# Chunk preparation, weight order and crossbar transposes in an attention and feed-forward kernel

## The chip, the cores and the metric

The kernel runs on 1 core of one Trainium2 chip. The metric is the device time of one execution in microseconds (us). Of each kernel, several executions were timed, one of them with a profile; the kernel before was run on the same chip beside every experiment.

## The reference, cut to what matters

```python
# q, k, v: (4, 8, 768, 64); heads 0, 2, 6 attend to everything before them,
# the five others to the first 4 tokens and a window of 64
scores = scale * np.matmul(q, k.transpose(0, 1, 3, 2))
scores = np.where(mask, scores, -1e9)
a = np.exp(scores - np.max(scores, axis=-1, keepdims=True))
a = a / (np.sum(a, axis=-1, keepdims=True) + 1e-09)
attn = np.matmul(a, v)
x = attn.transpose(0, 2, 1, 3).reshape(3072, 512)
h = x @ w_in                       # 512 x 2048
out = np.maximum(0.01 * h, h) @ w_out   # 2048 x 512
```

## The kernel before

The 3072 tokens are taken in 8 chunks of 384. For each chunk there is a preparation (k and q transposed), an attention that makes x, a first product with w_in ("product n", 16 ticks of four matmuls), and a second with w_out that makes the out tiles. A slot is a short piece of such work, a tick a slot of four matmuls. Slots of neighbouring chunks are merged, so that TensorE always has something to do; an empty slot only lets time pass. Everything is issued in program order; no scheduler moves it.

GpSimd issues nearly all loads from HBM (SyncE those of the first k, ScalarE a few values of v). SyncE issues transposes by the DMA crossbar, shifted copies of v, and the output. Chunks 1 and 2 are prepared by TensorE transposes; from chunk 3 on k and q go by the crossbar, six transposes in a row, followed by two shifts of v:

```python
def prep_dma(n):
    ...
    for g in range(3):
        nc.sync.dma_start_transpose(out=kt[i]...[:, :, tk], in_=kz[n % 2][:, g]...)      # k step
        nc.sync.dma_start_transpose(out=qts[n][:, :, t], in_=cast["q", n][:, g]...)      # q step
```

The buffers tie the two engines: `kz` has two buffers, so GpSimd may load k of chunk n + 2 only when the k steps of chunk n are through; `qb` has two as well. The main loop, and the choice of who transposes x:

```python
for n in range(2, NCH):
    a = []
    if n + 3 < NCH:
        load(n + 3)                       # GpSimd
    if n + 2 < NCH:
        prep_dma(n + 2)                   # SyncE: six transposes
        v_shift(n + 2, nc.sync)           # SyncE: two shifts
    if n + 1 < NCH:
        late = n + 1 > 3                  # x by crossbar from chunk 4 on
        a = Attention(n + 1, x_dma=late).slots()
        if late:
            a += [lambda: None] * (len(a) // 5)    # empty slots: time for the x transposes
    run(merge(merge(in_slots(n), outs) if outs else in_slots(n), a))
    ...
    outs = out_slots(n, ("py", "pt", "py") if n > 2 else ("py", "py", "py")) ...   # banks: buffers that TensorE writes
```

and the beginning:

```python
load(0, "v")
load_vb0()
masks()                      # GpSimd: eight small operations
for i in range(3):
    load_w("in", i)          # first weights
load(1)                      # k, q, v of chunk 1
load_w("in", 3)
...
in0 = in_slots(0, ("ph", "psS"))
run(in0[0:12])               # 12 ticks of the first product of chunk 0
for j, p in enumerate((0, 1, 3, 2)):
    prep_pair(1, p, ("py", "pt")[j % 2], "vva")    # TensorE transposes k and q of chunk 1
    ...
run(merge(out0[0:8], a1[16:] + [lambda: None] * 4))
```

The prediction counts the first product of chunk 0 as "product 1" where it speaks of the front; below, "product n" is that of chunk n, counted from 0.

The softmax here doesn't subtract the row's maximum and nothing guards it: scores larger than these inputs give would overflow.

Of the kernel before, what the change touches and what calls it, by code (L numbers as in the profile page):

```python
# [17 lines left out]
CH = 384  # L18
# [3 lines left out]
def kernel(  # L22
# [12 lines left out]
    nc = tc.nc  # L35
# [10 lines left out]
    NCH = B * (S // CH)  # L46
# [10 lines left out]
    def bank(tag, shape, dtype):  # L57
        return ps.tile(shape, dtype, name=tag, tag=tag, bufs=BANKS[tag])
# [19 lines left out]
    def load(n, nms="kqv"):  # L78

        b, c = divmod(n, 2)  # L80
        for nm in nms:
            if nm == "k" and n >= BY_DMA:

                for g in range(3):
                    for hh in range(2):
                        nc.gpsimd.dma_start(out=kz[n % 2][:, g, hh::2, D * hh : D * hh + D],  # L86
                                            in_=nat[nm][b, c, :, hh::2, g])
                continue
            if nm != "v":
                cast[nm, n] = rot.tile([128, 3, H, D], BF16, name=f"{nm}b", tag=f"{nm}b", bufs=2)  # L90
            for g in range(3):
                o = va[b % 2][:, 3 * c + g, :, 0:D] if nm == "v" else cast[nm, n][:, g]
                nc.gpsimd.dma_start(out=o, in_=nat[nm][b, c, :, :, g])  # L93

    def load_w(which, i):

        if which == "in":
            c = slice(512 * i, 512 * i + 512)
            nc.gpsimd.dma_start(out=w_in_bf[:, :, c], in_=w_in_r[:, :, c])
        else:  # L100
            c = slice(4 * i, 4 * i + 4)
            nc.gpsimd.dma_start(out=w_out_bf[:, c, :], in_=w_out_r[:, c, :])
# [5 lines left out]
    def bf(name, *shape):  # L108
        return one.tile([128, *shape], BF16, name=name)
# [4 lines left out]
    kt = [bf(f"kt{i}", 4, 2, S) for i in range(2)]  # L114
# [5 lines left out]
    kz = [bf(f"kz{i}", 3, H, 2 * D) for i in range(2)]  # L120
# [5 lines left out]
    def keep(m, pattern, comp, base, cm):  # L126
        nc.gpsimd.affine_select(out=m, in_=m, compare_op=comp, fill=0.0, base=base,
                                channel_multiplier=cm, pattern=pattern)

    def zeros(i, c):  # L130
        t = slice(CH * c, CH * c + CH)
        nc.vector.memset(kt[i][64:128, :, 0, t], 0.0)
        nc.vector.memset(kt[i][0:64, :, 1, t], 0.0)
# [5 lines left out]
    m_w = bf("m_w", 64)  # L139
    m_h = bf("m_h", H)  # L140

    def masks():
        nc.gpsimd.memset(m_caus[:], 1.0)
        keep(m_caus[:], [[1, 128]], ALU.is_ge, 0, -1)
        nc.gpsimd.memset(m_w[:], 1.0)
        keep(m_w[:], [[-1, 64]], ALU.is_gt, 0, 1)
        keep(m_w[:], [[1, 64]], ALU.is_ge, 64, -1)

        nc.gpsimd.memset(m_h[:], 1.0)
        keep(m_h[:], [[-NS, H]], ALU.is_ge, 0, 1)  # L150
        keep(m_h[:], [[NS, H]], ALU.is_ge, NS - 1, -1)
# [20 lines left out]
    def v_shift(n, eng=None):  # L172
        eng = eng or nc.scalar
        b, c = divmod(n, 2)
        i = b % 2
        lo, hi = (0, 2) if c == 0 else (2, 5)
        eng.dma_start(out=vb[i][0:64, lo:hi], in_=va[i][64:128, lo:hi])
        eng.dma_start(out=vb[i][64:128, lo:hi], in_=va[i][0:64, lo + 1 : hi + 1])

    def load_vb0():  # L180

        for t in range(2):
            nc.gpsimd.dma_start(out=vb[0][:, t, :, 0:D],
                                in_=v[0, :, 128 * t + 64 : 128 * t + 192, :].rearrange("h p d -> p h d"))

    def sink_keys(n, p, hh):
        b, c = divmod(n, 2)
        h = 2 * p + hh
        if c == 0 and not IS_RETR[h]:
            r = slice(64 * hh, 64 * hh + 64)  # L190
            nc.vector.tensor_copy(ksink[b % 2][r, p, NS * h : NS * h + NS], kt[b % 2][r, p, hh, 0:NS])

    def prep_pair(n, p, tag="pt", eng=("v", "v", "v")):
        b, c = divmod(n, 2)
        i = b % 2
        if p == 0:
            qts[n] = rot.tile([128, 4, CH], BF16, name="qt", tag="qt", bufs=2)
        pt = bank(tag, [128, 2, 4, 128], BF16)
        for e, nm in enumerate("kq"):
            for g in range(3):  # L200
                nc.tensor.transpose(pt[:, e, g, :], cast[nm, n][:, g, 2 * p : 2 * p + 2, :], ident[:])

        def move(e, dst, src):
            dst = dst.rearrange("p (g t) -> p g t", g=3)
            if e == "v":
                nc.vector.tensor_copy(dst, src)
            else:
                nc.scalar.activation(out=dst, in_=src, func=ACTF.Copy)

        for hh in range(2):  # L210
            r = slice(64 * hh, 64 * hh + 64)
            move(eng[hh], kt[i][r, p, hh, CH * c : CH * c + CH], pt[r, 0, 0:3, :])
            sink_keys(n, p, hh)
        move(eng[2], qts[n][:, p, :], pt[:, 1, 0:3, :])

    def prep_dma(n):
        b, c = divmod(n, 2)
        i = b % 2
        qts[n] = rot.tile([128, 4, CH], BF16, name="qt", tag="qt", bufs=2)
        for g in range(3):  # L220
            t = slice(128 * g, 128 * g + 128)
            tk = slice(CH * c + 128 * g, CH * c + 128 * g + 128)
            nc.sync.dma_start_transpose(out=kt[i].rearrange("p a e t -> p (a e) t")[:, :, tk],
                                        in_=kz[n % 2][:, g].rearrange("p h d -> p (h d)"))
            nc.sync.dma_start_transpose(out=qts[n][:, :, t], in_=cast["q", n][:, g].rearrange("p h d -> p (h d)"))

    def prep_first():

# [220 lines left out]
    py = {}  # L449

    def in_slots(n, tags=("ph",)):
        def tick(t):
            if t == 0:
                gs[n] = rot.tile([128, NG, CH], BF16, name="g", tag="g", bufs=2)
            ph = bank(tags[t % len(tags)] if t < 12 else "ph", [128, 512], FP32)
            for g in range(KG):
                nc.tensor.matmul(ph[:, 0:CH], lhsT=w_in_bf[:, g, 128 * t : 128 * t + 128],  # L457
                                 rhs=xts[n][:, g, :], start=(g == 0), stop=(g == KG - 1))
            nc.scalar.activation(out=gs[n][:, t, :], in_=ph[:, 0:CH], func=ACTF.Prelu, alpha=0.01)  # L459

        return [lambda t=t: tick(t) for t in range(NG)]
# [27 lines left out]
    def run(*lists):  # L489
        for l in lists:  # L490
            for f in l:
                f()

    def merge(ms, as_):

        r, done = [], 0
        for j, m in enumerate(ms):
            want = (j + 1) * len(as_) // len(ms)
            r += as_[done:want] + [m]
            done = want  # L500
        return r + as_[done:]
# [13 lines left out]
    nc.vector.memset(vb[0][:, 0:2, :, D], 1.0)  # L515
    zeros(0, 0)
    nc.vector.memset(ksink[0][:], 0.0)
    load(0, "v")
    load_vb0()
    masks()  # L520
    for i in range(3):
        load_w("in", i)
    load(1)
    load_w("in", 3)
    for a in ats:
# [16 lines left out]
    load(2)  # L542
    load(3)
    in0 = in_slots(0, ("ph", "psS"))
    run(in0[0:12])

    for j, p in enumerate((0, 1, 3, 2)):
        prep_pair(1, p, ("py", "pt")[j % 2], "vva")
        if j == 1:
            a1 = Attention(1, po_tags=("po", "po", "po", "ph")).slots(order=[0, 2, 6, 1, 3, 4, 5, 7])  # L550
        if j > 0:
            run(a1[j - 1 : j])
# [1 line left out]
    run(a1[3:8])  # L554
    run(merge(in0[12:], a1[8:16]))
    out0 = out_slots(0, ("py", "py", "py"))
    run(merge(out0[0:8], a1[16:] + [lambda: None] * 4))
    v_shift(2, nc.sync)
    load(4)
    prep_dma(3)  # L560
    v_shift(3, nc.sync)
    x = merge(in_slots(1), out0[8:])
    run(x[:8])
    a2 = [lambda j=j: prep_pair(2, j, ("pt", "psS")[j % 2]) for j in range(4)] + Attention(2).slots()
# [1 line left out]
    outs = []  # L566

    for n in range(2, NCH):
        a = []
        if n + 3 < NCH:  # L570
            load(n + 3)
        if n + 2 < NCH:
            prep_dma(n + 2)
            v_shift(n + 2, nc.sync)
        if n + 1 < NCH:

            late = n + 1 > 3
            a = Attention(n + 1, x_dma=late).slots()
            if late:
                a += [lambda: None] * (len(a) // 5)  # L580
        run(merge(merge(in_slots(n), outs) if outs else in_slots(n), a))
        if n + 2 < NCH:
            for h in range(H):
                sink_keys(n + 2, h // 2, h % 2)
        outs = out_slots(n, ("py", "pt", "py") if n > 2 else ("py", "py", "py")) if n + 1 < NCH else out_slots(n, ("psS", "psS", "py"), True)
    run(outs)


# [33 lines left out]
```

## Time and profile before

| | before |
|---|---|
| time, median of 3 runs | 246.09 us (244.64 to 246.15) |
| span of the profiled run | 243.0 us |
| TensorE busy | 224.3 us, 92% |
| mean granted TensorE clock | 0.993 |
| SyncE is through with chunk 4's transposes and shifts | 99.85 us |
| product 3 starts, without a wait | about 103.4 us |

The granted clock is the share of full speed that the profile records for TensorE. A half-clock window takes 3.41 us of records (19.1 to 22.6 us in this profile) and takes away half of that, 1.7 us of full clock, which is 0.7% of the span: 0.993 is one such window, 0.986 two, 0.98 three, 0.973 four. They do not fall alike in all executions of a kernel, which explains most of the spread of about 1.5 us: the runs of the kernel before average 244.6 us with no window, 245.5 with one and 246.0 with two (31 runs), so a window costs this kernel 0.5 to 1 us and not the full 1.7.

The groups of instructions of the page show the largest consumer of TensorE and the loads of k on GpSimd. After the form and the count stand busy time, mean ns of one, then the idle time just before them and what ended it:

```profile
L457 PE MATMUL ph<-xt,w_in_bf 128*128 128x384 bf16 x488 | 99.8, 328 | 0.0
...
L86 POOL DMA_DIRECT2D kz<-in_k_dram x30 | 22.5, 770 | 15.7 <-DMA kt<-kz 13.8
```

The first product never waits for its x (0.0 us). GpSimd waits 13.8 us in all for k transposes on SyncE to release `kz`. One line of GpSimd's timeline: start, duration, engine, line, operation, tiles, count, idle before it and what ended it.

```profile
115.52 1.48 POOL L86 DMA_DIRECT2D kz<-in_k_dram  x2 [3.21 <-DMA kt<-kz]
```

The third k step of chunk 5 leaves SyncE at 106.95 (SPq is SyncE's queue), and the last of the loads of k for chunk 7 go out at 115.52.

```profile
106.95 1.48 SPq L223 DMA_TRANSPOSE kt<-kz  x1
```

### The profile page before, as it was taken

How to read it: one execution, taken by the hardware profiler on the slowest of the kernel's cores; microseconds unless marked ns; L12 is line 12 of the kernel's file. 1: busy time of each engine (PE TensorE's matmuls, PEld its weight loads, DVE VectorE, ACT ScalarE, POOL GpSimd, SP SyncE). 2: the span in 40 equal slices, each digit the busy share in tenths (PEclk: the TensorE clock that was granted, in tenths of full speed). 3: DMA queues.
4: the chain of work that ended last, by engine and by line, in shares of the span. 5: the costliest groups of instructions: out<-in, count | busy, mean ns of one | idle time of the engine just before them, and what ended most of it. 6: DMA issues, size and time to landing. Idle time of an engine off the chain costs nothing.

```text
span 243.0 us, 4966 instructions
## 1 busy us (share of the span) xinstructions
PE 224.3 (92%) x1957; PEld 136.6 (56%) x1984; DVE 90.1 (37%) x257; ACT 131.6 (54%) x284; POOL 80.4 (33%) x108
## 2 busy tenths in 40 slices
PE   1778879989999999999999999999999999999994
PEld 0554546646665567565655666566556665455553
DVE  6888231714645324324421343234411352111121
ACT  2674688434664398766537665466447764333300
POOL 8994752679308962394370000000000000000000
PEclk9997999999999999999999999999999999999999
DMA  9999999999999999999999941676210111111112
GB/s 163 138 152 183 162 233 207 162 182 143 132 172 225 179 181 100 175 160 163 183 168 194 154 113 59 83 145 154 78 59 3 61 35 59 43 43 46 41 45 86
DMA packets 114858, 30.78 MB, mean 127 GB/s; under 512 B 105620, under 2 KB 110996, under 8 KB 114836
## 3 DMA queue, kind: packets, MB, share of 16 engines
q0 software_dynamic: 78304, 13.51, 79.0%
q1 hardware_dynamic: 36432, 16.95, 35.2%
q8 instruction: 15, 0.25, 0.4%
q14 instruction: 7, 0.06, 0.1%
q10 hardware_dynamic: 100, 0.02, 0.1%
HBM read 27.81 MB, written 6.29 MB: 140 GB/s over the span
## 4 chain that ended last, share of the span: by engine, by line
PE 86%; DVE 5%; ACT 3%; DMA 2%; issue 2%; POOL 1%; DVEq 0%; ACTq 0%; POOLq 0%
PE ph L457 31%; PE py L470 22%; PE po L296 6%; PE pt L470 6%; PE psS L329 6%; PE psS L470 4%; PE ph L470 3%; PE psS L365 2%; DMA qb<-in_q_dram 2%; PE psS L457 2%; DVE o L475 2%; PE psS L309 2%; DVE xs L402 1%; ACT at L334 1%; PE pt L411 1%
## 5 line engine op out<-in xcount | busy, mean ns | idle before, releaser
L457 PE MATMUL ph<-xt,w_in_bf 128*128 128x384 bf16 x488 | 99.8, 328 | 0.0
L459 ACT ACTIVATE g<-ph 128x384 bf16<-128x384 f32 x122 | 60.1, 492 | 57.5 <-PE ph L457 56.8
L470 PE MATMUL py<-w_out_bf,g 128*128 128x512 bf16 (+1 forms) x238 | 63.0, 371 | 1.5
L457 PEld LDWEIGHTS <-w_in_bf 128*128 128x128 bf16 x512 | 46.6, 99 | 30.8 <-issue 1.5
L470 PEld LDWEIGHTS <-g 128*128 128x128 bf16 x400 | 36.0, 97 | 28.3 <-issue 1.4
L334 ACT ACTIVATE at<-psS 128x384 bf16<-128x384 f32 x81 | 38.8, 491 | 12.4 <-PE psS L329 10.6
L329 PE MATMUL psS<-qt,kt 128*128 128x384 bf16 (+2 forms) x104 | 26.4, 295 | 2.4 <-ACT at L334 1.2
L93 POOL DMA_DIRECT2D qb<-in_q_dram x24 | 21.4, 912 | 21.9 <-DMA qt<-qb 9.9
L86 POOL DMA_DIRECT2D kz<-in_k_dram x30 | 22.5, 770 | 15.7 <-DMA kt<-kz 13.8
L475 DVE COPY o<-py 128x512 f32<-128x512 f32 (+1 forms) x16 | 10.8, 675 | 45.3 <-PE py L470 45.3
L93 POOL DMA_DIRECT2D va<-in_v_dram x24 | 21.3, 914 | 6.8 <-DMA w_in_bf<-in_moe_w_in_dram 3.3
L370 ACT ACTIVATE ats<-psS 128x384 bf16<-128x384 f32 x38 | 18.5, 492 | 4.8 <-PE psS L365 4.4
L296 PE MATMUL po<-va,at 128*128 128x65 bf16 x237 | 20.1, 194 | 0.3 <-DVE at L338 0.3
L296 PEld LDWEIGHTS <-at 128*128 128x128 bf16 x252 | 16.1, 99 | 7.5 <-DVE at L338 1.2
L402 DVE TENSOR_TENSOR xs<-po,linv 128x384 bf16<-128x384 f32 x30 | 16.7, 557 | 1.0
L470 PE MATMUL pt<-w_out_bf,g 128*128 128x512 bf16 x57 | 15.7, 379 | 0.4
L340 DVE TENSOR_TENSOR at<-at,m_caus 128x128 bf16<-128x128 bf16 x24 | 5.4, 224 | 28.5 <-ACT at L334 28.3
L329 PEld LDWEIGHTS <-kt 128*128 128x128 bf16 x108 | 10.6, 100 | 9.0 <-issue 1.6
L365 PEld LDWEIGHTS <-kt 128*128 128x128 bf16 x240 | 11.7, 98 | 5.2 <-issue 0.2
L296 PEld LDWEIGHTS <-ats 128*128 128x128 bf16 x240 | 11.5, 98 | 3.9 <-DVE ats L377 0.4
L338 DVE TENSOR_TENSOR at<-at,m_caus 128x256 bf16<-128x256 bf16 x24 | 7.0, 292 | 15.8 <-ACT at L334 15.5
L412 ACT ACTIVATE xt<-pt 128x384 bf16<-128x384 bf16 x14 | 6.9, 494 | 10.7 <-PE pt L411 10.7
(102 smaller groups left out, 195.0 us busy)
## 6 DMA issues: line engine op xcount, KB each, us to landing
out_dram<-o SPq DMA_DIRECT2D x23, 256.0 KB, 2.9
qb<-in_q_dram POOLq DMA_DIRECT2D x24, 128.0 KB, 6.6
va<-in_v_dram POOLq DMA_DIRECT2D x24, 128.0 KB, 7.3
w_in_bf<-in_moe_w_in_dram POOLq DMA_DIRECT2D x4, 512.0 KB, 8.3
w_out_bf<-in_moe_w_out_dram POOLq DMA_DIRECT2D x4, 512.0 KB, 13.7
kz<-in_k_dram POOLq DMA_DIRECT2D x30, 64.0 KB, 6.6
vb<-va SPq DMA_DIRECT2D x8, 195.0 KB, 5.9
vb<-va SPq DMA_DIRECT2D x6, 130.0 KB, 4.8
```

What stands on the lines that cost most here:

```text
L86: nc.gpsimd.dma_start(out=kz[n % 2][:, g, hh::2, D * hh : D * hh + D], in_=nat[nm][b, c, :, hh::2, g])
L93: nc.gpsimd.dma_start(out=o, in_=nat[nm][b, c, :, :, g])
L296: nc.tensor.matmul(o, lhsT=lhsT, rhs=rhs, start=first, stop=False, skip_group_check=True)
L329: nc.tensor.matmul(s[:, off : off + w], lhsT=kt[i][:, p, hh, 128 * kj : 128 * kj + 128], rhs=qts[n][:, p, lo:CH], start=(j == 0), stop=(j ...
L334: nc.scalar.activation(out=a[:, 0:off], in_=s[:, 0:off], func=ACTF.Exp, scale=SM)
L365: nc.tensor.matmul(s[:, 64 * m : 64 * m + 64], lhsT=kt[i][:, p, hh, k0 : k0 + 128], rhs=qts[n][:, p, 64 * m : 64 * m + 64], start=(m == 0) ...
L370: nc.scalar.activation(out=av_, in_=s[:, 0:CH].rearrange("p (j e f) -> p j e f", j=3, e=2), func=ACTF.Exp, scale=SM)
L402: nc.vector.tensor_tensor(xs[:], po[:, :, :, 0:D], linv.to_broadcast([128, 3, 2, D]), op=ALU.mult)
L457: nc.tensor.matmul(ph[:, 0:CH], lhsT=w_in_bf[:, g, 128 * t : 128 * t + 128], rhs=xts[n][:, g, :], start=(g == 0), stop=(g == KG - 1))
L459: nc.scalar.activation(out=gs[n][:, t, :], in_=ph[:, 0:CH], func=ACTF.Prelu, alpha=0.01)
L470: nc.tensor.matmul(py[n][:, 0 : c1 - c0], lhsT=gs[n][:, ng, 128 * tt : 128 * tt + 128], rhs=w_out_bf[:, ng, c0:c1], start=(ng == 0), stop= ...
L475: nc.vector.tensor_copy(o[:, 0 : c1 - c0], py[n][:, 0 : c1 - c0])
```

## The change

The intent: (A) bring the first weights earlier, by issuing them between the masks; (B) prepare chunk 1 between ticks of product 0, so that TensorE does not wait for the copies, with 6 in place of 4 empty slots later; (C) spread the crossbar transposes of k and q over the slots of the attention, where before all six stood ahead of it; (D) let the crossbar transpose x of chunk 3 too, which takes 12 transposes off TensorE and 4 copies off ScalarE, and use one more bank for out tiles of chunk 2.

```diff
-    def masks():
+    def mask_causal():
         nc.gpsimd.memset(m_caus[:], 1.0)
         keep(m_caus[:], [[1, 128]], ALU.is_ge, 0, -1)
+    def masks():
 ... prep_dma returns its steps (k, q, k, q, k, q, v shifts) and no longer issues them
+    mask_causal()
     load(0, "v")
     load_vb0()
+    load_w("in", 0)
     masks()
-    for i in range(3):
-        load_w("in", i)
+    load_w("in", 1)
+    load_w("in", 2)
     load(1)
 ...
-    run(in0[0:12])
+    run(in0[0:9])
     for j, p in enumerate((0, 1, 3, 2)):
         prep_pair(1, p, ("py", "pt")[j % 2], "vva")
+        run(in0[9 + j : 10 + j] if j < 3 else [])
 ...
-    run(merge(out0[0:8], a1[16:] + [lambda: None] * 4))
+    run(merge(out0[0:8], a1[16:] + [lambda: None] * 6))
 ... in the main loop
-        if n + 2 < NCH:
-            prep_dma(n + 2)
-            v_shift(n + 2, nc.sync)
         if n + 1 < NCH:
-            late = n + 1 > 3
+            late = n + 1 >= 3
             a = Attention(n + 1, x_dma=late).slots()
             if late:
                 a += [lambda: None] * (len(a) // 5)
+            if n + 2 < NCH:
+                for j, f in enumerate(prep_dma(n + 2)):
+                    a.insert(3 * j, f)
 ...
-        outs = out_slots(n, ("py", "pt", "py") if n > 2 else ("py", "py", "py")) ...
+        outs = out_slots(n, ("py", "pt", "py") if n >= 2 else ("py", "py", "py")) ...
```

More of the change, by code (lines that the diff above doesn't have):

```diff
@@ L219, in prep_dma, with k_step, q_step @@
         qts[n] = rot.tile([128, 4, CH], BF16, name="qt", tag="qt", bufs=2)
-        for g in range(3):
+        def k_step(g):
+            t = slice(CH * c + 128 * g, CH * c + 128 * g + 128)
+            nc.sync.dma_start_transpose(out=kt[i].rearrange("p a e t -> p (a e) t")[:, :, t],
+                                        in_=kz[n % 2][:, g].rearrange("p h d -> p (h d)"))
+        def q_step(g):
             t = slice(128 * g, 128 * g + 128)
-            tk = slice(CH * c + 128 * g, CH * c + 128 * g + 128)
-            nc.sync.dma_start_transpose(out=kt[i].rearrange("p a e t -> p (a e) t")[:, :, tk],
-                                        in_=kz[n % 2][:, g].rearrange("p h d -> p (h d)"))
             nc.sync.dma_start_transpose(out=qts[n][:, :, t], in_=cast["q", n][:, g].rearrange("p h d -> p (h d)"))
+        return [lambda f=f, g=g: f(g) for g in range(3) for f in (k_step, q_step)] + [lambda: v_shift(n, nc.sync)]
     def prep_first():
@@ L556 @@
     out0 = out_slots(0, ("py", "py", "py"))
-    run(merge(out0[0:8], a1[16:] + [lambda: None] * 4))
+    run(merge(out0[0:8], a1[16:] + [lambda: None] * 6))
     v_shift(2, nc.sync)
     load(4)
-    prep_dma(3)
-    v_shift(3, nc.sync)
+    run(prep_dma(3))
     x = merge(in_slots(1), out0[8:])
@@ L584 @@
                 sink_keys(n + 2, h // 2, h % 2)
-        outs = out_slots(n, ("py", "pt", "py") if n > 2 else ("py", "py", "py")) if n + 1 < NCH else out_slots(n, ("psS", "psS", "py"), True)
+        outs = out_slots(n, ("py", "pt", "py") if n >= 2 else ("py", "py", "py")) if n + 1 < NCH else out_slots(n, ("psS", "psS", "py"), True)
     run(outs)
```

## The prediction

> **What bounds the kernel now.** I read the page first (busy shares, the 40 slices, the chain that ended last), then a table of busy time by stage, then TensorE's timeline where the table shows it idle, then the timelines of the DMA queue on SyncE and of GpSimd. From the page:
>
> ```profile
> PE 224.3 (92%) x1957; PEld 136.6 (56%) x1984; DVE 90.1 (37%) x257; ACT 131.6 (54%) x284; POOL 80.4 (33%) x108
> PE   1778879989999999999999999999999999999994
> PEclk9997999999999999999999999999999999999999
> DMA  9999999999999999999999941676210111111112
> PE 86%; DVE 5%; ACT 3%; DMA 2%; issue 2%; POOL 1%; DVEq 0%; ACTq 0%; POOLq 0%
> ```
>
> TensorE works 92% of the span and is 86% of the chain. Its holes are in the first six or seven slices and the last. The DMA engines are full until about slice 22, then nearly idle: a second resource that can bound the first 135 us. The same by stage (us; busy and count of TensorE, weight loads, VectorE, ScalarE, GpSimd; granted clock; DMA share; GB/s):
>
> ```profile
> 5.40:19.50 14.10, 10.10 (x135) 7.68 (x136) 11.09 (x37) 8.81 (x18) 13.27 (x22) 0.99 1.66 152
> 19.50:28.80 9.30, 9.30 (x51) 5.25 (x49) 4.45 (x9) 5.84 (x12) 5.62 (x7) 0.84 2.15 165
> 28.80:36.50 7.70, 5.26 (x63) 3.49 (x61) 3.36 (x10) 6.07 (x15) 4.26 (x5) 1.00 1.33 222
> 36.50:51.00 14.50, 13.34 (x156) 8.65 (x156) 6.33 (x18) 8.99 (x21) 7.54 (x10) 1.00 1.87 179
> 82.60:103.00 20.40, 19.82 (x222) 13.20 (x222) 7.59 (x25) 17.41 (x42) 9.85 (x13) 1.00 1.88 158
> 128.50:229.50 101.00, 99.80 (x809) 58.60 (x824) 27.88 (x76) 54.94 (x118) 0.00 (x0) 1.00 0.43 79
> ```
>
> TensorE is idle 4.0 us in the first row (attention of chunk 0), 2.4 in the third (preparation of chunk 1), 1.2 in the fourth, 0.6 in the fifth, 1.2 in the 101 us of the last: after 51 us nothing but less TensorE work can help much. TensorE in the third row:
>
> ```profile
> 28.81 0.33 PE L201 MATMUL py<-ident,kb 128*128 128x128 bf16 x3
> 30.71 0.32 PE L329 MATMUL psS<-qt,kt 128*128 128x384 bf16 x1 [1.06 <-ACT qt L208]
> 33.14 0.32 PE L329 MATMUL psS<-qt,kt 128*128 128x384 bf16 x1 [0.89 <-ACT at L334]
> 33.91 0.33 PE L329 MATMUL psS<-qt,kt 128*128 128x256 bf16 x2 [0.35 <-ACT at L334]
> ```
>
> TensorE transposes k and q of chunk 1, then waits for the copies of VectorE and ScalarE. The DMA queue on SyncE, and GpSimd waiting for its transposes, in the stage that prepares chunk 4:
>
> ```profile
> 84.65 1.36 SPq L223 DMA_TRANSPOSE kt<-kz  x1
> ...
> 92.47 4.25 SPq L223 DMA_TRANSPOSE kt<-kz  x1
> 96.82 1.75 SPq L225 DMA_TRANSPOSE qt<-qb  x1
> 98.67 0.53 SPq L177 DMA_DIRECT2D vb<-va  x1
> 99.30 0.55 SPq L178 DMA_DIRECT2D vb<-va  x1
> 99.95 1.28 SPq L223 DMA_TRANSPOSE kt<-kz  x1
> ```
>
> ```profile
> 99.54 1.48 POOL L86 DMA_DIRECT2D kz<-in_k_dram x2 [6.87 <-DMA kt<-kz]
> 102.47 1.48 POOL L86 DMA_DIRECT2D kz<-in_k_dram x2 [1.45 <-DMA kt<-kz]
> ```
>
> The six transposes of chunk 4 keep SyncE for 14 us (84.65 to 98.57); GpSimd's waits show the second k transpose (88.18) landed near 99.0 and the third (92.47) near 101.9. Attention of chunk 4 starts at 103.24, so these are barely in time.
>
> **What the Trainium skill says.** "DMA: Bandwidth & Descriptors", section "Issuing engines are not separate DMA queues": DMAs from SyncE, ScalarE and GpSimd all run on the same 16 engines and interleave. The trace agrees: an x transpose issued among GpSimd's loads at 113 us landed after 8.9 us, those after 195 us in 2.3. "Perfetto Trace Analysis", section "Per-instruction lifecycle": data movement lies outside a DMA's profiled bar; so I use landings and waits, not bars. "TensorE: Matmul & The Clock Gate", section "Part 1: The HAM clock gate": the array runs at half clock after an idle window of about 3.4 us until activity releases it. The trace agrees in kind: clock 0.84 in the second row, where the chain shows four matmuls of product 1 at 1.28 us, later 0.65.
>
> **The change, part by part.**
>
> First weights. GpSimd issues v at 5.20 to 7.87, vb until 9.62, then spends 1.9 us on masks before the first weights at 11.53. Now m_caus (about 0.55 us) goes before v, and the first weights follow vb at about 10.2 instead of 11.5. v and vb land 0.55 us later: the second stream unit of chunk 0 may wait a few tenths, but a wait on VectorE (0.25 us, sink values) stands there anyway. Product 1 starts at 19.5 on a wait for VectorE, with its weights there since 16.9 (issue 11.53, 5.4 to land): no direct gain. The gain is behind: GpSimd's loads are one backlog from here on (the q loads of chunk 1 take 10.4 us each to land), so they come 0.8 to 1.3 us earlier.
>
> Chunk 1 between ticks. The last q load of chunk 1 is issued at 18.1 and lands at 28.5, just before its transposes at 28.8. Three ticks of product 1 (3 x 0.65 = 1.95 us) move behind the start of the preparation, which could thus start at 26.9; but q now lands near 27.5 (28.5 less 0.8 to 1.3). So the chain copy, exp, score starts about 1.0 us earlier, and the ticks fill the 1.06 and 0.89 us waits. ScalarE takes 3 more results of 0.49 us there, in idle time it had (0.66 + 0.26 + 0.43 us). I take 0.9 us. The padding of product 2 (6 in place of 4 empty slots) spreads the x transposes of chunk 1 at 44 to 50 us, where TensorE waits 0.58 and 0.23: 0.5 us.
>
> x of chunk 3. Twelve TensorE transposes go (56 ns apart: 0.7 us), 4 ScalarE copies (2.0 us) in a stage where ScalarE is 85% busy, and the waits of 0.30 and 0.23 us that the timeline shows before 99.7 and 101.8. With 0.7 + 0.5 us about 1.3 us of TensorE's time (0.1 for ScalarE's relief, a guess), if x is there when needed. Added: 4 crossbar transposes on SyncE's queue.
>
> Spread transposes. Where instructions stand in SyncE's queue is all that spreads them. The order for chunk 4 becomes k q k q k, x, q, two v shifts, three x. Nothing in front of the first five holds them back, so they start as before and the x transposes stand behind a queue that is 12 to 15 us long.
>
> Sum without a new wait: -0.9 - 0.5 - 1.3 = -2.7, with 0.3 guessed for out tiles in "pt" (chunk 2): -3.0 us, 243.1.
>
> **The rivals.**
>
> (a) Everything lands in time: 243.1, up to 4.5 us gained if the preparation fills better. For it: the last x is finished some 2.5 us before the end of the stage (padding of a fifth), and free x transposes take 2.3 us.
>
> (b) x of chunk 3 arrives late, product 3 waits. On the old time axis, SyncE is through with six transposes and the shifts at 99.85; one x in between (1.18 us) makes it 101.0, three more 104.6; the last, issued at 103.4, lands after 2.3 us at best (105.7), after 4 to 5 more likely (107.5). Product 3 wants it at 103.4 less the 3 us gained. The queue itself moves earlier by only 1 to 2 us. So TensorE waits 3 to 6 us, and all gains before are eaten: net 0 to +3 us, 246 to 249; a wait that long may also drop the clock for one 3.4 us window (up to +1.7). Against it: GpSimd's traffic is light near 100 us, since its loads wait for the transposes. I hold this likelier (60%).
>
> (c) The first weights delay v, and attention of chunk 0 waits: at most 0.5 us.
>
> (d) x between k and q steps in later stages delays chunk 5's k and q: they are needed 15 us later, so nothing.
>
> **Range and chances.** 0.4 x 243.1 + 0.6 x 248.0 = 246.0. The runs of the kernel before spread over 1.5 us. 8 in 10: 242.0 to 249.5. Faster by 2% would be below 241.2, which takes (a) and more: 0.10. Slower by 2% is above 251.0: (b) with a dropped clock: 0.07.
>
> **What would show it.** First weights: issue near 10.2, q of chunk 1 landed near 27.5. Preparation: the first score of chunk 1 before 29.7, the waits of 1.06 and 0.89 gone, tick 13 near 35.5 (was 36.5). x: no transposes of xs on TensorE near 83 to 103 but that of chunk 2; the last x transpose of chunk 3 on SyncE's queue after 100; and a TensorE wait of 3 us or more before the first matmul of product 3, with the x transfer as releaser. If that wait is missing, (a) holds and I am some 3 us too high. If the preparation is no shorter, the landing of q did not move.

## The result, and the profile after

The changed kernel took 256.37 us (median of 258.12, 256.94, 255.79 and 253.23); the kernel before, in the same rounds, 246.12. A ratio here is the mean time of one kernel's fast runs over that of the other's fast runs of the same rounds, so it is not quite the ratio of the medians. It is 1.0386, with a 95% interval of 1.0277 to 1.0495: **9.5 us slower** (255.32 against 245.83). That is above the top of the predicted range, 249.5.

The profiled execution is the one of 258.12 us, which counts as slow, being over 1.5% above the fastest: it has four half-clock windows (clock 0.973), the three others two or three (0.98 to 0.987). Its mechanisms are read below, and the profiled runs of e1, e2, e4 and e5, all fast, show one or the other of its two waits; its sizes at half clock are those of the worst run. From the page after:

```profile
PE   1869789799999999299994999999999999999995
...
PEclk9997999999999999959999799999999999999999
...
PE 70%; DMA 15%; POOL 6%; ACT 2%; issue 2%; DVE 2%; SPq 2%; POOLq 0%
...
L465 PE MATMUL ph<-xt,w_in_bf 128*128 128x384 bf16 x488 | 101.6, 332 | 8.4 <-DMA xt<-xs 8.4
...
L86 POOL DMA_DIRECT2D kz<-in_k_dram x30 | 22.4, 767 | 28.8 <-DMA kt<-kz 26.3
```

TensorE's row has two new holes (2 in the 17th slice, 4 in the 22nd), each followed by a low digit of the clock (5, 7). The share of DMA in the chain that ended last rose from 2% to 15%. The first product, which never waited for x, now waits 8.4 us, and GpSimd's wait for k transposes doubled, from 13.8 to 26.3 us. TensorE before product 3 and before product 4:

```profile
104.00 0.34 PE L465 MATMUL ph<-xt,w_in_bf 128*128 128x384 bf16 x1 [0.61 <-DMA xt<-xs]
106.80 0.32 PE L465 MATMUL ph<-xt,w_in_bf 128*128 128x384 bf16 x1 [2.45 <-DMA xt<-xs]
...
140.85 0.32 PE L465 MATMUL ph<-xt,w_in_bf 128*128 128x384 bf16 x1 [3.68 <-DMA xt<-xs]
```

The first four matmuls of product 3 wait one after the other for the four transfers of x of chunk 3 (the two that are left out for 0.44 and 1.17 us), and product 4 waits for the last of chunk 4.

Following the first and the last result of each product in both traces splits the 13.4 us of these two executions. The front, up to the end of product 1, loses 0.72. The stage of product 2 gains 0.74, because TensorE no longer transposes x of chunk 3. The start of product 3 then loses 5.33 by the wait, and its ticks 2.64 at half clock (107.8 to 114.6 us). The start of product 4 loses 3.84, its ticks 1.66 at half clock (141.9 to 145.3). From there to the end the two run alike. The sum is 0.72 - 0.74 + 5.33 + 2.64 + 3.84 + 1.66 = 13.45 us.

SyncE's queue after, ahead of the second wait:

```profile
109.79 1.43 SPq L226 DMA_TRANSPOSE kt<-kz  x1
118.71 0.34 SPq L484 DMA_DIRECT2D out_dram<-o  x1
121.03 1.18 SPq L412 DMA_TRANSPOSE xt<-xs  x1
122.73 1.56 SPq L231 DMA_TRANSPOSE qt<-qb  x1
124.40 1.24 SPq L226 DMA_TRANSPOSE kt<-kz  x1
...
131.90 2.70 SPq L412 DMA_TRANSPOSE xt<-xs  x1
```

and GpSimd's last loads of k for chunk 7 in the same trace:

```profile
128.12 1.48 POOL L86 DMA_DIRECT2D kz<-in_k_dram  x2 [8.10 <-DMA kt<-kz]
```

After 109.79 + 1.43 SyncE issues nothing for 7.5 us: next in its queue stands an output, whose tile VectorE has not copied yet. Behind it stand an x transpose, a q step, and only then the third k step of chunk 5, at 124.40 (106.95 before). That step releases `kz`: the loads of k for chunk 7 go out at 128.12 (115.52 before), those of q and v behind them at 130.1 to 135.4. The last x of chunk 4, issued at 131.90 as soon as its data were there (131.88), is in flight with them and lands at 140.81, after 8.9 us.

So the theory after this reading: x of chunk 3 is late because its four transfers stand behind six transposes and are slow among GpSimd's loads; x of chunk 4 is late because the spread order delays the k steps and, through the buffers, GpSimd's loads, which then meet x; and half clock follows the idleness. The rivals: (A) or (B) do it by shifting everything; the two waits are one cause; SyncE's queue alone is late, whatever the loads do; the half clock is chance. Twelve kernels test this.

### The profile page after: what moved, and what is told of

Read it like the earlier page. It is cut to its first block, busy times and chain, and to the rows that moved or that the text cites. A ratio compares the mean times of both kernels' runs of the same rounds, so it can differ in the third digit from the quotient of the medians.

```text
span 256.2 us, 4946 instructions
## 1 busy us (share of the span) xinstructions
PE 229.1 (89%) x1944; PEld 137.5 (54%) x1972; DVE 90.0 (35%) x257; ACT 129.6 (51%) x280; POOL 80.1 (31%) x108
## 4 chain that ended last, share of the span: by engine, by line
PE 70%; DMA 15%; POOL 6%; ACT 2%; issue 2%; DVE 2%; SPq 2%; POOLq 0%
PE ph L465 25%; PE py L478 18%; PE pt L478 6%; PE po L304 5%; DMA xt<-xs 5%; PE psS L337 5%; DMA qb<-in_q_dram 4%; PE psS L478 3%; DMA kt<-kz 3%; PE ph L478 3%; DMA kz<-in_k_dram 3%; PE psS L373 2%; POOL qb L93 2%; PE psS L317 1%; DVE o L483 1%
## 5 line engine op out<-in xcount | busy, mean ns | idle before, releaser
L465 PE MATMUL ph<-xt,w_in_bf 128*128 128x384 bf16 x488 | 101.6, 332 | 8.4 <-DMA xt<-xs 8.4
L478 PE MATMUL py<-w_out_bf,g 128*128 128x512 bf16 (+1 forms) x221 | 60.2, 381 | 2.2 <-DVE o L483 0.8
L478 PEld LDWEIGHTS <-g 128*128 128x128 bf16 x400 | 36.6, 99 | 30.3 <-issue 3.9
L86 POOL DMA_DIRECT2D kz<-in_k_dram x30 | 22.4, 767 | 28.8 <-DMA kt<-kz 26.3
L337 PE MATMUL psS<-qt,kt 128*128 128x384 bf16 (+2 forms) x104 | 27.4, 303 | 1.7 <-ACT at L342 1.2
L93 POOL DMA_DIRECT2D qb<-in_q_dram x24 | 21.3, 905 | 17.4 <-DMA qt<-qb 10.2
L483 DVE COPY o<-py 128x512 f32<-128x512 f32 (+1 forms) x15 | 10.1, 674 | 42.5 <-PE py L478 40.4
L478 PE MATMUL pt<-w_out_bf,g 128*128 128x512 bf16 x73 | 20.0, 379 | 0.3
L373 PE MATMUL psS<-qt,kt 128*128 128x64 bf16 x228 | 13.0, 194 | 0.0
L304 PE MATMUL po<-va,ats 128*128 128x65 bf16 x129 | 12.4, 194 | 0.0
```

The source lines that it names most:

```text
L86: nc.gpsimd.dma_start(out=kz[n % 2][:, g, hh::2, D * hh : D * hh + D], in_=nat[nm][b, c, :, hh::2, g])
L93: nc.gpsimd.dma_start(out=o, in_=nat[nm][b, c, :, :, g])
L304: nc.tensor.matmul(o, lhsT=lhsT, rhs=rhs, start=first, stop=False, skip_group_check=True)
L337: nc.tensor.matmul(s[:, off : off + w], lhsT=kt[i][:, p, hh, 128 * kj : 128 * kj + 128], rhs=qts[n][:, p, lo:CH], start=(j == 0), stop=(j ...
L373: nc.tensor.matmul(s[:, 64 * m : 64 * m + 64], lhsT=kt[i][:, p, hh, k0 : k0 + 128], rhs=qts[n][:, p, 64 * m : 64 * m + 64], start=(m == 0) ...
L465: nc.tensor.matmul(ph[:, 0:CH], lhsT=w_in_bf[:, g, 128 * t : 128 * t + 128], rhs=xts[n][:, g, :], start=(g == 0), stop=(g == KG - 1))
```

## The experiments

### Which part does it

**e1_x3_tensor**: the changed kernel without the crossbar for x of chunk 3 (A, B, C; the bank for out tiles of chunk 2 stays).

```diff
-            late = n + 1 >= 3
+            late = n + 1 > 3
```

> The change with x of chunk 3 back on TensorE, the spread order of SyncE's queue kept. Theory 'late x' (the four crossbar transposes of chunk 3 are the whole cause, and the second wait, before product 4, is only an echo of the first): both waits go, 246 to 247.5 us. Rival 'queue order' (k and q steps of chunk 5 stand behind x and out transfers that wait for VectorE, so the loads of chunk 7 come late and collide with x of chunk 4): the wait before product 4 stays at 3 to 4 us, with a stretch at half clock after it, 250 to 252 us.

251.94 us (250.97 to 253.43), ratio 1.0254 [1.0196, 1.0312]. The wait before product 3 is gone. The wait before product 4 remains (4.3 us, until 135.2), with one half-clock window behind it.

**e2_front**: the changed kernel with all k and q steps in front again (A, B, D).

```diff
+        if n + 2 < NCH:
+            run(prep_dma(n + 2))
...
-            if n + 2 < NCH:
-                for j, f in enumerate(prep_dma(n + 2)):
-                    a.insert(3 * j, f)
```

> The change with all k, q and v steps of a chunk in front of its stage again, x of chunk 3 still by crossbar. 'Late x': the wait before product 3 stays at 4 to 6 us and is followed by a half-clock stretch; if the second wait is an echo of the first it stays too, 253 to 257 us. 'Queue order': the first wait stays, the second goes, 249 to 251.5 us.

254.33 us (252.37 to 256.43), ratio 1.0374 [1.0296, 1.0453]. Now the wait before product 3 is there (2.2 and 1.2 us, and 1.7 us for q of chunk 4 ahead of them), with two half-clock windows behind it, and none before product 4. The waits are those that "queue order" foretold, the time is above its 249 to 251.5.

**e3_both_undone**: both edits (A, B; the bank stays).

> The change with the spread order and x of chunk 3 both undone: what is left are the first weights between the masks, the preparation of chunk 1 between ticks, 6 empty slots and the out tiles of chunk 2. Both theories: no wait of over 1 us after 60 us. From the trace of the changed kernel, whose product 1 of chunk 1 starts 0.7 us later than before: 246.5 to 247.2 us. If the prediction's gain of 1.4 us from these parts is real: 244.7.

247.71 us (247.12 to 248.14), ratio 1.0075 [1.0032, 1.0118]. Neither wait. What is left of the change costs 2.0 us, more than either expectation: TensorE waits for q of chunk 1 three times in the preparation, 0.4, 0.65 and 0.8 us long. The windows are not the reason, since the run that had none took 247.1 us, against 244.6 on average before.

The two waits are two causes. Each part alone on the kernel before says the same:

**e4_x3_alone**: the kernel before with D.

```diff
-            late = n + 1 > 3
+            late = n + 1 >= 3
...
-        outs = out_slots(n, ("py", "pt", "py") if n > 2 else ...
+        outs = out_slots(n, ("py", "pt", "py") if n >= 2 else ...
```

> The kernel before with x of chunk 3 by crossbar (with its padding of the stage, and the out tiles of chunk 2) as the only change. 'Late x': a wait of 4 to 6 us before product 3 and a half-clock stretch, 250 to 252 us, and more if the second wait follows. If the queue only fills up in company with the other parts: 245 to 246.5 us.

252.6 us (251.34 to 253.83), ratio 1.0275 [1.022, 1.0331]: 7.0 us, a little above the expected 250 to 252. In its trace the stage of product 2 is 0.95 us shorter, product 3 starts 5.2 us late (so its start loses 6.1 us), and ends 7.8 late.

**e5_spread_alone**: the kernel before with C.

```diff
-        if n + 2 < NCH:
-            prep_dma(n + 2)
-            v_shift(n + 2, nc.sync)
...
+            if n + 2 < NCH:
+                for j, f in enumerate(prep_dma(n + 2)):     # k, q, k, q, k, q, shifts
+                    a.insert(3 * j, f)
```

> The kernel before with the spread order of SyncE's queue as the only change. 'Queue order' (the second and third k step of chunk 5 stand behind an out and an x transfer that wait for VectorE; GpSimd's k loads of chunk 7 wait for those k steps, so the q and v loads of chunk 7 come about 2 to 5 us late, in the time of the last x transfer of chunk 4): one wait of 3 to 5 us before product 4 and a half-clock stretch, none before product 3, 250 to 252 us. If the spread hurts only in company with the first parts of the change: 245.5 to 247 us.

251.15 us (249.29 to 253.54), ratio 1.0268 [1.0209, 1.0326]. The three fast runs average 250.5 against 245.4 before, which makes 5.1 us; the recorded ratio is higher, and one of the four runs counts as slow (253.54). The wait is 3.8 us, before product 4 only, with a half-clock window behind it (131.6 to 135.0).

The parts do not simply add up: A and B 2.0, C 5.1, D 7.0 make 14.1 us, the whole change costs 9.5. No run here says how they offset each other.

### Is it the place of the k steps?

**e6_k_front**: as e5, but the three k steps go in front and only the q steps and the shifts are spread. If the route is k step, buffer, load, x, the loss must go.

```diff
-                for j, f in enumerate(prep_dma(n + 2)):
-                    a.insert(3 * j, f)
+                st = prep_dma(n + 2)
+                run([st[0], st[2], st[4]])
+                for at, f in ((2, st[1]), (7, st[3]), (12, st[5]), (15, st[6])):
+                    a.insert(at, f)
```

> The spread order alone, but with the three k steps of a chunk in front of its stage; q steps, v shifts, x and out transfers interleaved as in the change. 'Queue order by way of the k loads': GpSimd's loads of chunk 7 come as early as in the kernel before or earlier, the wait before product 4 goes or falls under 1.5 us, 245.5 to 247.5 us. Rival (the x transfers of chunk 4 are late because q steps and v shifts stand in front of them, and the loads are innocent): the wait stays at 3 to 5 us, 249.5 to 252 us.

245.31 us (245.02 to 246.77), ratio 1.0009 [0.9972, 1.0046]: 4.9 of the 5.1 us are back. The third k step of chunk 5 leaves SyncE at 104.37; in e5 it left at 114.95, after an output at the head of the queue had waited 4.4 us for VectorE and an x transpose behind it 1.8 us (before: 106.95). That k step, the last loads of k for chunk 7 on GpSimd, and TensorE before product 4, in e5:

```profile
114.95 3.19 SPq L224 DMA_TRANSPOSE kt<-kz  x1
...
122.25 1.48 POOL L86 DMA_DIRECT2D kz<-in_k_dram  x2 [8.12 <-DMA kt<-kz]
...
132.28 0.48 PE L463 MATMUL ph<-xt,w_in_bf 128*128 128x384 bf16 x1 [3.84 <-DMA xt<-xs]
```

and the loads and TensorE in e6:

```profile
113.92 0.74 POOL L86 DMA_DIRECT2D kz<-in_k_dram  x1 [0.28 <-DMA va<-in_v_dram]
...
131.24 0.32 PE L463 MATMUL ph<-xt,w_in_bf 128*128 128x384 bf16 x1 [1.14 <-DMA xt<-xs]
```

In e5 GpSimd waits 8.1 us for the k step, as it does in the changed kernel; in e6 other loads hold it, not the k step, and these loads are 8 us earlier. The first half of the route is shown. The second half is not shown: in e6's profiled run (246.77 us, its slowest) the last x still took 7.2 us to land, among the loads of q for chunk 7, and 1.1 us of wait before product 4 remained, with no half-clock window; in e5 the last x, issued 1.2 us later, took about as long. The wait fell by 2.7 us (1.0 because x landed sooner, 1.7 because TensorE came later, 1.0 of it after a wait for q of chunk 4), and the half-clock window fell away with it. The rival that SyncE's queue alone is late has a part in e5: its last x stood in the queue for 2.2 us after its data were there (122.91 to 125.12), in e6 for none. In the changed kernel and in e1 the queue held it under 0.2 us, and it was in flight for 8.9 and up to 9.6 us, against 4.3 to 6.9 in e2, e4, e7 and e8, where the k steps stand in front. That fits contention, but no run takes the loads of chunk 7 away. So e6 shows that the order of the k steps costs the time, and not by which transfers it makes the last x late.

### Why is x of chunk 3 late?

**e7_k4_early**: e4, with chunk 4's three k steps issued one stage earlier, so that less stands in front of x in the queue.

```diff
+    last = x.pop()
+    x.append(lambda: (last(), k_steps(4)))
...
-            prep_dma(n + 2)
+            prep_dma(n + 2, n == 2)      # without its k steps
```

> The kernel before with x of chunk 3 by crossbar, and the three k transposes of chunk 4, two thirds of what stood in front of the x transposes, issued before the last three out transfers of product 1, some 10 us earlier. 'Late x is queue time': the x transposes of chunk 3 are issued by 100 us, the wait before product 3 falls to under 1.5 us, 245 to 246.5 us. Rival (crossbar transposes among GpSimd's loads are slow by themselves, wherever they stand): the wait stays over 3 us, 250 to 252 us.

249.6 us (248.34 to 250.0), ratio 1.0163 [1.0128, 1.0199]: 3.0 us of D's 7.0 are taken back. The last x left SyncE at 98.46 (e4: 104.15), as soon as its data was there, and still landed only near 106; TensorE waited 3.8 us. So the queue is a part of it, and an x that leaves in time is late all the same. This run fell between the two expectations.

**e9_no_loads**: e4 without GpSimd's loads of k and v of chunk 5 and k of chunk 6. The result is wrong (relative error 0.296).

```diff
+            if (nm, n) in (("k", 5), ("v", 5), ("k", 6)):
+                continue
```

> The kernel before with x of chunk 3 by crossbar (252.6 us), without GpSimd's k and v loads of chunk 5 and its k loads of chunk 6 (a wrong result on purpose: old data are used); the order of SyncE's queue is the same. If the wait before product 3 comes from the crossbar transposes sharing the DMA engines with GpSimd's loads: the six transposes of chunk 4 leave SyncE in 9 to 11 us instead of 14, x of chunk 3 lands 2 to 4 us after its issue, the wait falls under 1.5 us, 244 to 246 us. If it comes from the order and number of SyncE's own transfers alone: the wait stays over 3 us, 250 to 252.5 us.

249.01 us (248.05 to 249.49), ratio 1.0147 [1.0111, 1.0184]. SyncE got rid of the six transposes in 9 us where the kernel before needs 14, and all x left by 100.8. But the loads of q and v of chunk 6, no longer held up, moved forward and met the x transfers. TensorE still waited 3.7 us. It neither confirmed nor refuted contention, since one set of loads had taken the place of another.

**e12_fewer_loads**: e9 without those loads either (chunk 6 takes q of chunk 5; wrong, relative error 0.58).

```diff
+            if (nm, n) in (("k", 5), ("v", 5), ("k", 6), ("q", 6), ("v", 6)):
+                if nm == "q":
+                    cast["q", 6] = cast["q", 5]
+                continue
```

> x of chunk 3 by the crossbar alone, with GpSimd's loads of k and v of chunk 5 and of k, q and v of chunk 6 all left out (chunk 6 takes the q of chunk 5; wrong result on purpose), so that no load should be in flight between about 85 and 108 us. Theory 'contention': the lateness of x of chunk 3 comes from its transfers sharing the engines with GpSimd's loads. Then the four x transposes leave SyncE from about 95 us, land within 3 us each, the wait before product 3 (2.0 + 2.0 us with the loads that were left over, 4.7 to 5.2 with all) falls below 1.5 us, no half clock follows, and the time is 244.5 to 246.5 us. Theory 'queue': the four x transposes with six transposes and two shifts in front of them, and their own dependence on VectorE, are late by themselves. Then 3 us or more of wait remain and the time stays at 248 to 250.

242.82 us (242.6 to 243.63), ratio 0.9927 [0.9898, 0.9957]. The loads of chunk 6 on GpSimd in e9:

```profile
95.75 2.63 POOL L95 DMA_DIRECT2D qb<-in_q_dram  x3 [13.94 <-DMA qt<-qb]
98.34 2.66 POOL L95 DMA_DIRECT2D va<-in_v_dram  x3
```

and TensorE in e9 at the beginning of product 3:

```profile
105.17 0.32 PE L459 MATMUL ph<-xt,w_in_bf 128*128 128x384 bf16 x1 [1.86 <-DMA xt<-xs]
107.31 0.32 PE L459 MATMUL ph<-xt,w_in_bf 128*128 128x384 bf16 x1 [1.82 <-DMA xt<-xs]
```

GpSimd's first loads after 84 us in e12:

```profile
104.96 1.49 POOL L90 DMA_DIRECT2D kz<-in_k_dram  x2 [21.95 <-DMA kt<-kz]
```

and TensorE in e12 where product 3 begins, with no wait in brackets:

```profile
101.63 0.33 PE L333 MATMUL psS<-qt,kt 128*128 128x384 bf16 x1
101.79 0.85 PE L461 MATMUL ph<-xt,w_in_bf 128*128 128x384 bf16 x4
```

In both kernels the four x transposes leave SyncE between 95 and 101 us. With six loads beside them (95.75 to 101.0) TensorE waits 3.7 us; with none it does not wait, no half-clock window follows, and D saves what it was meant to: 0.96 us in the stage of product 2 (the shift against before goes from -0.66 to -1.62 and stays). The lateness of x of chunk 3 is contention with the loads. It acts twice: on the x transfers, and on the transposes in front of them, which keep SyncE 14 us in the kernel before and 10 us here. A miss in the expectation: the one landing that the trace has came 4.2 us after issue where under 3 were expected, so this transfer was slower than 2.3 us among transposes too, only still in time; and the time came out below the expected 244.5, of which 0.66 us was gained at the front, where this profiled run had no half-clock window.

### Does the half clock come from the idleness?

**e8_warm**: e4 with 16 useless matmuls into a free bank before product 3.

```diff
+        if n == 3:
+            warm = bank("ph", [128, 512], FP32)
+            for _ in range(16):
+                nc.tensor.matmul(warm[:], lhsT=w_in_bf[:, 0, 0:128], rhs=w_in_bf[:, 0, 0:512], start=True, stop=True)
```

> The kernel before with x of chunk 3 by crossbar (252.6 us) and 16 useless matmuls of 512 columns (about 3.5 us) put into TensorE's wait before product 3. If the half clock after the wait comes from TensorE's idle time: the clock stays full after product 3 starts, product 3 still starts 5 us late, and the time falls by the 2.6 us that product 3 lost after its start, to 250.0. If the clock drops for another reason: 252.6 or more.

249.82 us (249.48 to 250.63), ratio 1.0186 [1.0157, 1.0215]; about 2.5 us less than e4 against the kernel before. The same two stretches of e4 (busy time and count of TensorE, weight loads, VectorE, ScalarE, GpSimd; granted clock; DMA share; GB/s):

```profile
100.00:107.50 7.50, 3.33 (x17) 1.45 (x16) 0.45 (x3) 2.22 (x5) 4.46 (x6) 1.00 1.76 165
107.50:115.00 7.50, 6.46 (x28) 3.06 (x28) 1.26 (x4) 1.85 (x4) 3.78 (x5) 0.54 1.99 162
```

and the second of them in e8, where TensorE was busy 6.47 us in the first:

```profile
107.50:115.00 7.50, 6.42 (x55) 3.92 (x55) 1.51 (x6) 3.66 (x8) 3.52 (x5) 1.00 1.91 168
```

In e4 TensorE is busy 3.33 of the first 7.5 us and then runs at a clock of 0.54: 28 matmuls. In e8 it is kept busy, the clock stays at 1.00, and 55 matmuls pass in the same time. All four runs of e8 have a mean clock of 0.992 to 0.999, those of e4 0.973 to 0.980. Product 3 starts about as late (4.7 us against the kernel before, 5.2 in e4), and only 0.5 us more is lost behind it, at a wait before product 4. The half clock is a consequence of the wait, not chance.

### The front

**e10_masks_alone**: the kernel before with A, in 5 rounds.

```diff
+    mask_causal()
     load(0, "v")
     load_vb0()
+    load_w("in", 0)
     masks()
-    for i in range(3):
-        load_w("in", i)
+    load_w("in", 1)
+    load_w("in", 2)
```

> The kernel before with the order of masks and first weights on GpSimd as the only change. The prediction: the loads behind come 0.8 to 1.3 us earlier; with the preparation of chunk 1 where it was that is worth 0 to 0.3 us. From the changed kernel's trace: q of chunk 1 lands within 0.2 us of where it did, time the same within 0.3%. Rival: v and vb, 0.35 us later, make attention of chunk 0 wait, 0.3 to 0.5 us slower.

246.51 us (245.48 to 248.12), ratio 1.0059 [1.002, 1.0098]: 1.3 us slower. The first weights were issued at 10.07 (11.53 before) and landed at 17.87 (16.98 before); the last q of chunk 1 landed at 29.09 (28.52 before). TensorE waited 0.65 us for it. The loss is larger than any expectation, and not all of it need come from the order: this profiled run has two half-clock windows at the front (31.5 to 38.3) where the kernel before has one, and the three runs with one window average 246.4 us against 245.7 for such runs of the kernel before in the same rounds.

In this trace the earlier issue, into DMA engines that the page shows full, landed nothing earlier: the first weights came 0.9 us later, and k and q of chunk 1 behind them 0.5 to 0.6 us later. Why the whole backlog moved, no run shows.

**e11_q_first**: the kernel before with k and q of chunk 1 ahead of the third piece of w_in, v of chunk 1 after it, and four ticks of product 0 between the steps of the preparation.

```diff
-    for i in range(3):
+    for i in range(2):
         load_w("in", i)
-    load(1)
+    load(1, "kq")
+    load_w("in", 2)
+    load(1, "v")
...
-    run(in0[0:12])
+    run(in0[0:8])
... after the third and fourth pair, and after a1[2] and a1[3]: one tick each
```

> A version of the second part of the change that gives it what it waited for: the kernel before with k and q of chunk 1 loaded before the third piece of w_in, and the preparation of chunk 1 after tick 8, with ticks 9 to 12 between its steps. If the early preparation failed only because q of chunk 1 had not landed: no wait for q, scores of chunk 1 some 2.5 us earlier, 1 to 2 us faster than before. If ScalarE's added results in that stage eat it: same within 0.3%. If the third piece of w_in comes too late for tick 9: 0.5 to 1 us slower.

243.98 us (243.12 to 244.57), ratio 0.9943 [0.9913, 0.9974]: **1.4 us faster than the kernel before**, with a correct result, and the only correct kernel that beats both. The last q of chunk 1 landed at 24.86. TensorE there:

```profile
25.50 0.33 PE L201 MATMUL py<-ident,kb 128*128 128x128 bf16 x3
25.67 0.33 PE L201 MATMUL py<-ident,qb 128*128 128x128 bf16 x3
```

The preparation starts at 25.5, and its q transposes at 25.67 have no wait in front of them. The first score of chunk 1 comes at 27.39 (30.71 before). In the interleaving of part B the idea was right. What it lacked was that q had to be there, and for that the order of the loads had to change, not the time of their issue. Two things changed together here, so their shares are not told apart. Nor is the whole 1.4 us theirs for certain: five of the six runs had no half-clock window at the front, four of the eleven of the kernel before. Between the runs without a window the gain is 0.8 us (243.8 against 244.5), and whether the change itself keeps the clock up no run shows.

## Why the prediction was wrong

It said 246.0 us and gave 7% to slower by over 2%; the kernel is 3.9% slower.

**The step that failed most is rival (d)**: "x between k and q steps in later stages delays chunk 5's k and q: they are needed 15 us later, so nothing". It asked when the transposed k is needed, and did not ask what its source buffer, once free, sets going. In e5, where nothing else had been late until then, the third k step of chunk 5 left 8.0 us later (114.95 for 106.95), `kz` came free later, and the last loads of k for chunk 7 went out 6.7 us later (122.25 for 115.52). In the changed kernel, where the wait before product 3 comes on top, it is 17.5 and 12.6 us. Order alone costs 5.1 us (e5), and with the k steps in front again 0.2 (e6). That is shown; that the later loads are what delays the last x of chunk 4 is argued from their timing, and part of its delay in e5 is SyncE's queue itself (2.2 us).

**Rival (b) had the right mechanism for chunk 3, and its size was too small.** It put the last x transpose of chunk 3 at SyncE at 103.4 (measured 105.16), foresaw a wait of 3 to 6 us (the start of product 3 lost 5.3 us in the trace after and 6.1 in e4, of which TensorE waited 4.7 for x in both), and gave "net 0 to +3 us". Two terms of its sum were mis-sized. The gains that were to be set against the wait were 3 us and are at most 1.0 (x of chunk 3: 0.74 here, 0.95 in e4 and 0.96 in e12, where 1.3 were counted; the front below zero). And half clock was "one 3.4 us window (up to +1.7)", while the runs show up to two windows, 2.6 us. So even its worst case, 249 and 1.7, stayed below every run of the changed kernel. "GpSimd's traffic is light near 100 us" was the argument against (b), and the runs refute it: in the changed kernel GpSimd issued six loads of k between 94.1 and 105.7, and in e9 with e12 six loads issued in the 5 us around the x transposes are the whole of a 3.7 us wait.

**The steps on the front failed too.** The first weights were issued at 9.93, near the 10.2 foretold, but landed at 17.59 in place of 16.98, and q of chunk 1 landed at 28.40, not 27.5. The prediction carried an earlier issue over to an earlier landing, at a time when its own view showed the DMA engines full. Preparation "0.9 us" and padding "0.5 us" were to gain 1.4 us, and up to the end of product 1 the trace loses 0.72: the start of the first score moved from 30.71 to 30.15, not below 29.7, because TensorE now waits for q itself, and A and B together cost 2.0 us in e3 (A alone 1.3 in e10, windows included). Of the padding no run was made alone; the trace shows TensorE waiting 0.78 us for VectorE's copy of an out tile before 50.2 us, and whether six slots are the cause is open. The view that was read as a wait for copies (1.06 and 0.89 us) was right as it stood, but taking away one wait uncovered the next.

**Right** were the sign of part D on TensorE's own work, that the queue on SyncE decides whether x of chunk 3 is in time, and the test that the prediction named: a wait of 3 us or more before product 3, with the x transfer as its releaser. No such test was set for product 4.

## What to carry to other kernels

Before spreading or reordering transfers in an in-order queue, ask of each not only when its result is needed, but which buffer it frees, who waits to refill it, and what that refill may then collide with. With the DMA engines full, issuing earlier did not land earlier here (e10); putting the needed transfer ahead of another did (e11). A wait of TensorE of some 4 us brought 1.7 us of half clock behind it (one window) or 2.6 (two), so a rival that ends in such a wait deserves more than the wait itself.

## What the Trainium skill lacked or had wrong

- "DMA: Bandwidth & Descriptors", section "Issuing engines are not separate DMA queues", says that all DMAs interleave on the same 16 engines. The runs agree, but it has no figure of what that does to a small transfer: an x transpose landed 2.3 us after issue with little beside it, and 8.9 us among GpSimd's loads; six loads beside four x transposes made 3.7 us of wait (e9), none made none (e12). The section calls the sequencer's time to initiate a DMA usually small relative to the DMA itself; here an x transpose kept SyncE for 1.2 of the 2.3 us to its landing, and six transposes kept it for 14 us among loads and 10 us without them.
- "VectorE: DVE Perf Modes", section "The three transpose paths", gives 390 ns on TensorE and 1309 ns by the DMA crossbar for a 128x128 transpose. It gives no figure beside other traffic: here an x transpose, three such blocks, kept SyncE for 1.2 us and landed 2.3 to 8.9 us after issue, and moving it from TensorE cost 7.0 us among loads (e4) and saved 1.0 without them (e12).
- "TensorE: Matmul & The Clock Gate", section "Part 1: The HAM clock gate", names an idle window of about 3.4 us. The runs agree in kind, but the window need not be all idle. The part also tells of short idles between groups of matmuls that make the clock go up and down, without a size: in the 3.41 us before each drop from product 3 on, TensorE was idle for 2.1 (e9) to 3.2 us (e5), in part with single matmuls between, and 1.7 idle did not trip it (e4, 101.1 to 104.5). The price was two windows where a further wait for x of 0.7 to 1.2 us fell into the first (e2, e4, the wait before product 3 in after), and one elsewhere (e1, e5, e7, e9, product 4 in after); 16 matmuls, 3.6 us in all, were enough to prevent it (e8).
- No page has the route by which the order in SyncE's queue reaches GpSimd: an output waiting 4.4 us for its data at the head of the queue, a k step behind it 8.0 us later than before, a buffer, and loads 6.7 us later (e5).
- No page says that with a backlog of loads the landing does not follow the issue: the first weights issued 1.5 us earlier landed 0.9 us later (e10, one trace).
